# Three early expert rounds inside linear attention, resident weights and per-chunk gathers in a top-2 mixture-of-experts kernel

## The chip, the cores and the metric

The kernel runs on one core of one Trainium2 chip. The metric is device time in microseconds, lower is better. A median is given with the number of runs. A run is called slow when it is over 1.5% above the fastest of the same kernel; the ratios use the other runs, the fast ones.

## The reference, cut to what matters

```python
# attention: q, k, v of 8 batches x 8 heads x 576 x 64, phi(x) = elu(x) + 1
kv  = einsum('bhsd,bhse->bhde', phi(k), v);  z = sum(phi(k), axis=2)
x   = einsum('bhsd,bhde->bhse', phi(q), kv) / (einsum('bhsd,bhd->bhs', phi(q), z) + 1e-6)
x   = x.transpose(0, 2, 1, 3).reshape(4608, 512)
# noisy top-2 router over 8 experts, then the experts
noisy = x @ w_gate + log1p(exp(x @ w_noise)) * noise
top2, top2_w = the two best experts of each row and the softmax of their two values
for e in range(8):                                  # w1: 512 x 1024, w2: 1024 x 512
    out[rows of e] += weight * (relu(x[rows of e] @ w1[e]) @ w2[e])
```

Each of 4608 rows goes to two experts, so there are 9216 visits. The kernels give each expert ten tiles of 128 rows (1280 places), and a branch for overflow.

## The kernel before

It has two stages. The **attention stage** goes over four groups of two batches: cast loads of k, v, q on GpSimd, phi on ScalarE and VectorE, products and transposes on TensorE, routing (one step of it is the **ranking**, a few matmuls that give each row its place within its expert), and a **dispatch**: 18 scatters (indirect DMAs, issued by GpSimd) that write each row of x, with a few routing numbers, to the places of its two experts in the DRAM tensor `x_sorted`.

```python
# PhaseA.route, end: "dispatch"
for ci in range(NC):                 # 9 blocks of 128 rows
    for sl in range(2):              # first and second expert of a row
        r = nc.gpsimd.indirect_dma_start(out=self.x_sorted,
            out_offset=bass.IndirectOffsetOnAxis(ap=posi[:, ci, sl : sl + 1], axis=0),
            in_=xrow[:, ci, :].bitcast(INT32), in_offset=None)
```

The **expert stage** takes each expert's ten tiles in chunks of 4, 4 and 2. The two experts of a row both have to add into the same row of `out`. The second one to come therefore gathers what the first one wrote (called **L**), adds its own part while it empties the matmul bank, and scatters the sum. A gather may start only when all scatters of earlier experts have landed.

```python
# PhaseB.run; pools: 3 weight sets, 4 xt, 2 hT, 12 L, 6 y; PSUM 4 banks h, 3 banks y
for e in range(E):
    gate, si, gi = self.meta(...)                 # row data: where to gather and to scatter
    for n in (512, 512, 256):                     # a chunk: up to 4 tiles
        nc.sync.dma_start(out=xt[:, :, 0:n], in_=self.x_sorted[...], transpose=True)
        hT = self.mm1(w1, xt, n)                  # 32 matmuls, 8 ReLUs
        if prev is not None:
            flush(prev)                           # chunk before: 8 matmuls, y = ps*gate + L, scatter
        if t0 == 0:
            if e + 3 < E: self.load_w(e + 3)      # 4 loads of 512 KB, on GpSimd
            for t in range(T_CAP):
                L[t] = self.gather(gi[:, t : t + 1]) if e > 0 else None
        prev = {...}
```

## Time and profile before

| | before |
|---|---|
| time, median of 3 (range) | 583.14 us (580.96 to 592.49) |
| span of the first trace (a run of 597.23 us, 2.8% above the fastest of the three) | 595.4 us |
| attention stage, to the end of the last dispatch | 243.7 us |
| from there to the end | 351.7 us |
| TensorE busy, whole span | 373.5 us (63%) |

In the lines of the profile, L and a number is a source line, `a<-b` says what an instruction writes and reads, x and a number is a count. In a group the numbers after the bar are busy time in us and the mean of one instruction in ns; after the second bar stands how long the engine had idled just before these instructions, and what ended most of it. In a list of waits the three numbers are us in total, times, and the longest. In a timeline they are the start and the length in us, with the idle time before in brackets. In a table by stage, each engine's busy us and its instructions follow the stretch.

### The profile page before, as it was taken

Reading aid. Unit: us, or ns where it says so; the run is one execution under the profiler, and the core shown is the slowest. Engines: PE = TensorE matmul, PEld = TensorE weight load, DVE = VectorE, ACT = ScalarE, POOL = GpSimd, SP = SyncE. Lnnn points to the kernel's source line nnn. Section 1 sums busy time; section 2 is a strip of 40 time slices with the busy share of each in tenths; the row PEclk is TensorE's granted clock in tenths of the full one; section 3 lists DMA queues with packets and bytes.
Section 4 is the critical chain, followed back from the end, with each engine's and each line's share of the span. In section 5 each row is a group of like instructions: output and inputs, shape, how many; then the busy total and the mean of one; then the engine's idle time right before and its main releaser. Section 6 shows DMA issues by size and latency. Waiting matters only on the chain. (4 is left out here: it accounts for less than half of the span.)

```text
span 595.4 us, 5833 instructions
## 1 busy us (share of the span) xinstructions
PE 373.5 (63%) x1976; PEld 194.5 (33%) x1976; DVE 221.8 (37%) x638; ACT 170.2 (29%) x265; POOL 288.7 (48%) x315
## 2 busy tenths in 40 slices
PE   0173173137245300199989928969948968989984
PEld 0151142015124100045444404425424434444442
DVE  4359655375650560413233104314304304333122
ACT  0466444025021120062333401421511321423410
POOL 6445378427427117204346516725706726565364
PEclk9996555556555555589999978998987998998998
DMA  9999954995602002555864993993893995573153
GB/s 168 210 191 191 191 131 101 192 209 157 124 27 102 36 10 106 128 91 130 184 101 121 184 110 80 228 140 101 217 120 101 243 146 145 189 157 145 57 160 128
DMA packets 122985, 82.65 MB, mean 139 GB/s; under 512 B 74164, under 2 KB 108980, under 8 KB 122944
## 3 DMA queue, kind: packets, MB, share of 16 engines
q0 software_dynamic: 65888, 69.02, 56.8%
q1 hardware_dynamic: 54272, 12.98, 14.8%
q10 hardware_dynamic: 2784, 0.18, 0.4%
q8 instruction: 17, 0.28, 0.2%
q14 instruction: 24, 0.20, 0.1%
HBM read 80.72 MB, written 32.87 MB: 191 GB/s over the span
## 5 line engine op out<-in xcount | busy, mean ns | idle before, releaser
L474 PE MATMUL h_ps<-xt,w 128*128 128x512 bf16 (+1 forms) x768 | 150.5, 355 | 39.5 <-DMA xt<-x_sorted 32.3
L476 ACT ACTIVATE hT<-h_ps 128x512 bf16<-128x512 f32 (+1 forms) x192 | 99.4, 527 | 260.8 <-PE h_ps L474 209.2
L483 PE MATMUL y_ps<-w,hT 128*128 128x512 bf16 x640 | 149.8, 392 | 36.5 <-DVE y L489 36.5
L490 POOL DMA_INDIRECT out_dram<-y,si x80 | 79.4, 992 | 97.4 <-DVE y L487 39.9
L474 PEld LDWEIGHTS <-w 128*128 128x128 bf16 x768 | 77.8, 101 | 111.1 <-issue 46.9
L376 POOL DMA_INDIRECT x_sorted<-xrow,posi x72 | 73.6, 1022 | 78.9 <-DVE xrow L373 33.7
L461 POOL DMA_INDIRECT L<-out_dram,gi x70 | 70.6, 1009 | 82.1 <-DMA out_dram<-y,si 60.6
L483 PEld LDWEIGHTS <-hT 128*128 128x128 bf16 x640 | 64.1, 100 | 115.5 <-issue 45.3
L489 DVE SCALAR_TENSOR_TENSOR y<-y_ps,gate,L 128x512 f32<-128x512 f32 x70 | 51.1, 731 | 98.8 <-PE y_ps L483 60.6
L460 DVE MEMSET L<- 128x512 f32 x70 | 34.0, 485 | 34.4 <-DMA x_sorted<-xrow,posi 24.4
L270 PE MATMUL num_ps<-kvbd,pqt 128*128 128x162 bf16 x128 | 22.2, 324 | 38.6 <-DVE lwt L293 34.6
L203 PE MATMUL kv_ps<-v,phk 128*128 128x192 bf16 x128 | 26.0, 360 | 19.0 <-DVE phk L190 19.0
L335 PE MATMUL kv_ps<-A,ut 128*128 128x72 bf16 x4 | 0.9, 219 | 44.2 <-DVE A L331 44.2
L270 PEld LDWEIGHTS <-pqt 128*128 128x128 bf16 x128 | 13.2, 130 | 45.6 <-DVE lwt L293 41.3
L248 ACT COPY pqt<-t_ps 128x1024 bf16<-128x1024 bf16 x16 | 16.0, 1014 | 32.5 <-PE t_ps L244 10.6
L287 DVE TENSOR_TENSOR xrow<-num_ps,rden 128x512 bf16<-128x512 f32 x36 | 24.7, 687 | 0.5
L444 DVE SCALAR_TENSOR_TENSOR isf<-meta 128x10 f32<-128x10 f32 x8 | 1.4, 174 | 58.5 <-DMA meta<-x_sorted 58.5
L203 PEld LDWEIGHTS <-phk 128*128 128x128 bf16 x128 | 14.1, 131 | 23.6 <-DVE phk L190 19.0
L244 PE MATMUL t_ps<-ident,phq 128*128 128x128 bf16 x128 | 16.0, 306 | 8.0 <-ACT pqt L248 4.5
L185 ACT ACTIVATE e<-kt 128x2048 bf16<-128x2048 bf16 x8 | 15.2, 1912 | 10.7 <-DMA kt<-in_k_dram 7.9
L487 DVE TENSOR_SCALAR y<-y_ps,gate 128x512 f32<-128x512 f32 x10 | 7.5, 750 | 28.7 <-PE y_ps L483 28.7
L244 PEld LDWEIGHTS <-phq 128*128 128x128 bf16 x128 | 13.7, 144 | 9.2 <-issue 9.2
(116 smaller groups left out, 277.2 us busy)
## 6 DMA issues: line engine op xcount, KB each, us to landing
w<-in_moe_w_dram POOLq DMA_DIRECT2D x32, 512.0 KB
kt<-in_k_dram POOLq DMA_DIRECT2D x8, 512.0 KB
v<-in_v_dram POOLq DMA_DIRECT2D x8, 512.0 KB
qt<-in_q_dram POOLq DMA_DIRECT2D x8, 512.0 KB
x_sorted<-zrow SPq DMA_DIRECT2D x8, 264.0 KB, 6.6
out_dram<-y,si POOLq DMA_INDIRECT x80
x_sorted<-xrow,posi POOLq DMA_INDIRECT x72
L<-out_dram,gi POOLq DMA_INDIRECT x70
```

Source lines behind the costliest of these rows:

```text
L203: nc.tensor.matmul(out=ps[:, i, 0:192], lhsT=phk[:, hp, ci, :], rhs=vt[:, hp::4, 64 * ci : 64 * ci + 64], start=(i == 0 and ci == 0), stop ...
L244: nc.tensor.transpose(tp[:, i * 512 + ci * P : i * 512 + ci * P + P], phq[:, 2 * half + i, ci, :], c["ident"][:],)
L270: nc.tensor.matmul(out=ps[:, hp, 0:KVW], lhsT=pqs[j][:, hp, cc * P : cc * P + P], rhs=kvbds[j][:, hp, :], start=(hp % 2 == 0), stop=(hp % ...
L287: nc.vector.tensor_tensor(out=_ap(xrow[:, ci, 0:HD], [[64, 4], [256, 2], [1, 64]]), in0=_ap(ps, [[256, 4], [64, 2], [1, 64]]), in1=_ap(rd, ...
L376: r = nc.gpsimd.indirect_dma_start(out=self.x_sorted, out_offset=bass.IndirectOffsetOnAxis(ap=posi[:, ci, sl : sl + 1], axis=0), in_=xrow[ ...
L460: nc.vector.memset(L[:], 0.0)
L461: nc.gpsimd.indirect_dma_start(out=L[:].bitcast(INT32), out_offset=None, in_=self.out.bitcast(INT32), in_offset=bass.IndirectOffsetOnAxis( ...
L474: nc.tensor.matmul(out=ps[:, 0:n], lhsT=w1[:, dc, fc * P : fc * P + P], rhs=xt[:, dc, 0:n], start=(dc == 0), stop=(dc == 3))
L476: nc.scalar.activation(out=hT[:, fc, 0:n], in_=ps[:, 0:n], func=ACT.Relu)
L483: nc.tensor.matmul(out=ps[:], lhsT=hT[:, fc, t * P : t * P + P], rhs=w2[:, fc, :], start=(fc == 0), stop=(fc == 7))
L489: nc.vector.scalar_tensor_tensor(out=y[:], in0=ps[:], scalar=gate, in1=L[:], op0=ALU.mult, op1=ALU.add)
L490: r = nc.gpsimd.indirect_dma_start(out=self.out, out_offset=bass.IndirectOffsetOnAxis(ap=si, axis=0), in_=y[:], in_offset=None, bounds_che ...
```

## The change

The attention stage leaves TensorE mostly idle. The change wants to put expert work there: after three of six smaller routing units an **early round** does two tiles of each of experts 0 to 3, whose weights are loaded early and stay in SBUF. 24 of the 80 tiles move, and 56 are left for the **late stage**. To make room, the late stage also changes: L is gathered chunk by chunk into fewer buffers, there are two buffers for transposed rows (xt) and four for y, the second matmuls of a chunk are spread between the first matmuls of the next, and the weights of experts 4 to 6 are loaded when attention has ended. In attention the odd rows (512 to 575 of each head) are loaded on SP in fp32, and ScalarE's function table is loaded once.

```diff
+UNITS = [(0, 0, 4), (0, 4, 9), (1, 0, 9), (2, 0, 9), (3, 0, 4), (3, 4, 9)]
+ROUNDS = [(1, 256), (2, 512), (3, 768)]          # after unit 1, 2, 3; rows up to this bound
+    nc.scalar.preload_act_table_set(ACT_SET)
 ...  (PhaseB: pools)
-        self.wp = ctx.enter_context(tc.tile_pool(name="B_w", bufs=3))
-        self.xp = pool("B_x", 4)
-        self.lp = pool("B_l", 12)
-        self.yp = pool("B_y", 6)
+        self.wp = [pool("B_w", E1)]               # E1 = 4
+        self.xp = pool("B_x", 2)
+        self.lp = [pool("B_l", 3)]                # 3 more in the late stage
+        self.yp = [pool("B_y", 2)]                # 2 more in the late stage
 ...  (one chunk of an expert)
-                hT = self.mm1(w1, xt, n)
-                if prev is not None:
-                    flush(prev)
-                if t0 == 0:
-                    if e + 3 < E:
-                        self.load_w(e + 3)
-                    for t in range(T_CAP):
-                        L[t] = self.gather(gi[:, t : t + 1]) if e > 0 else None
+            self.mm1(w1, xt, hT, n, range(0, 2))
+            for i in range(1, 4):
+                want = -(-k * i // 4)
+                while done < want:
+                    self.tail(prev, done)         # second matmuls, y, scatter of the chunk before
+                    done += 1
+                self.mm1(w1, xt, hT, n, range(2 * i, 2 * i + 2))
+            while done < k: ...
+            L = {}
+            if not first:
+                for t in range(t0, t0 + n // P):
+                    L[t] = self.gather(gi[:, t : t + 1])
 ...  (main)
+        def early(i):
+            lo = ROUNDS[i - 1][1] if i else 0
+            for e in range(E1):
+                pb.expert(e, lo, (ROUNDS[i][1] - lo) // P, col(c["cnt"][i], e), i == 0 and e == 0, f"read{i}")
+            pb.flush()
+            if b < 2:
+                with tc.issue_after(pa.last_load):
+                    for e in ([0], [1, 2, 3])[b]:
+                        pb.load_w(e)
+            while unit < len(UNITS) and ...:
+                pa.route(unit)
+                for i, (after, _) in enumerate(ROUNDS):
+                    if after == unit:
+                        early(i)
+                unit += 1
+    for e in range(E1, 7):
+        pb.load_w(e, 1)
+    for e in range(E):
+        r0 = row0 if e < E1 else 0
+        pb.expert(e, r0, T_CAP - r0 // P, col(carry, e), False)
+        if e == 0:
+            pb.load_w(7)
```

## The prediction

> **What bounds the kernel now.** I read the engine table in 40 slices first, then busy time by stage (I cut the span at the four moments at which a group's ranking matmuls run and at the first expert matmul), then the groups, the waits, and the chain that ended last.
>
> ```profile
> PE   0173173137245300199989928969948968989984
> PEclk9996555556555555589999978998987998998998
> DMA  9999954995602002555864993993893995573153
> ```
>
> The attention half (slices 0 to 16) has TensorE mostly idle at half clock; the expert half has it nearly full. DMA is full only to about 75 us and again at 104 to 134 us, where the first three experts' weights load.
>
> ```profile
> core 0: us, PE busy (x) PEld busy (x) DVE busy (x) ACT busy (x) POOL busy (x), PEclk, DMA share, GB/s
> 0.00:72.40 72.40, 19.62 (x144) 13.24 (x145) 42.83 (x128) 32.23 (x29) 35.15 (x55) 0.84 1.45 190
> 72.40:128.00 55.60, 20.56 (x144) 13.43 (x143) 28.48 (x97) 17.19 (x18) 32.24 (x34) 0.50 0.89 154
> 128.00:171.90 43.90, 20.01 (x144) 12.84 (x143) 26.46 (x89) 12.53 (x14) 20.73 (x20) 0.54 0.56 123
> 171.90:218.90 47.00, 20.48 (x142) 13.16 (x140) 20.21 (x78) 8.82 (x12) 17.43 (x18) 0.50 0.14 52
> 218.90:251.10 32.20, 0.00 (x0) 0.01 (x1) 6.87 (x38) 0.00 (x0) 17.32 (x18) 0.50 0.35 99
> 251.10:595.40 344.30, 292.81 (x1408) 141.83 (x1408) 96.95 (x211) 99.41 (x192) 165.84 (x170) 0.92 0.68 143
> ```
>
> So: four attention groups of 72, 56, 44 and 47 us, no engine full, bound by chains from engine to engine (and by DMA in the first); 32 us in which only the last group's rows are scattered, TensorE at zero; then 344 us of experts, where TensorE is 293 us busy.
>
> ```profile
> L483 PE MATMUL y_ps<-w,hT 128*128 128x512 bf16 x640 | 149.8, 392 | 36.5 <-DVE y L489 36.5
> L490 POOL DMA_INDIRECT out_dram<-y,si x80 | 79.4, 992 | 97.4 <-DVE y L487 39.9
> L376 POOL DMA_INDIRECT x_sorted<-xrow,posi x72 | 73.6, 1022 | 78.9 <-DVE xrow L373 33.7
> L461 POOL DMA_INDIRECT L<-out_dram,gi x70 | 70.6, 1009 | 82.1 <-DMA out_dram<-y,si 60.6
> L489 DVE SCALAR_TENSOR_TENSOR y<-y_ps,gate,L 128x512 f32<-128x512 f32 x70 | 51.1, 731 | 98.8 <-PE y_ps L483 60.6
> PE y_ps L483 <- DVE y L489: 36.5, 6, 12.9
> POOL L L461 <- DMA out_dram<-y,si: 60.6, 6, 16.1
> ```
>
> An expert's partial results (L) may be gathered only when the scatters before have landed; 36.5 of TensorE's 51 idle us in the expert stage are that wait. In the chain that ended last, one of them is
>
> ```profile
> 473.96 8.41 DMA out_dram<-y,si
> ...
> 500.56 6.91 PE y_ps L483 x32
> ```
>
> The first line is a scatter issued just behind a weight load. Where no load is ahead, the timeline has a scatter landed 2.3 us after its issue ends, and a gather too. The second is the dense rate: 6.91/32 = 216 ns per 512-column matmul.
>
> **What the Trainium skill says.** "TensorE: Matmul & The Clock Gate", Part 1 and "Back-to-back issue gap": half rate by default and again after an idle window of about 3.4 us; N/2.4 + 2.5 ns warm. The trace agrees: 0.50 in attention, 216 ns when dense. "DMA: Bandwidth & Descriptors", "Issuing engines are not separate DMA queues": all queues use the same 16 engines, another issuer saves only issue time. No run here shows it yet. Same page, "Two DMAs through the same engine are not ordered": in one queue descriptors start in order; the 8.41 against 2.3 us fits a scatter queued behind a weight load. "ScalarE: Activation LUTs", "What ACT_TABLE_LOAD costs": about 1283 ns for the load itself; the trace has nine loads of 1283 ns.
>
> **The change, part by part.**
>
> *Expert work moved.* A tile of 128 rows costs 32 x 128 + 8 x 512 = 8192 columns, 16 x 216 ns = 3.45 us warm. There were and are 80 tiles. Three rounds x 4 experts x 2 tiles = 24 run early, 56 x 3.45 = 193 us remain. Removed from the late stage: 24 x 3.45 = 83 us.
>
> *Work added to the attention half.* POOL: 24 scatters and 22 gathers at 1.27 us (0.97 busy plus 0.3 between) = 58 us. DVE: 24 evictions x 0.75 = 18 us, 12 row-data blocks of nine instructions of about 0.17 = 18 us, two more routing units at some 9 us = 18 us; fewer, larger divisions give about 10 back. ACT: 96 ReLUs at 0.385 = 37 us and 22 zero copies at about 0.6 = 13 us, less eight table loads (10 us). Moving 24 odd-row loads from POOL to SP frees 24 x 0.7 = 17 us of POOL. DMA: 16 weight loads where 12 were; a 512 KB load at some 200 GB/s (209 in the slice at 119 us, nearly all weights) takes 2.6 us, so 42 us of queue, now in front of batches 3 and 4. No engine fills, but chains lengthen.
>
> *The new chain.* Two tiles per expert and round, one output bank, and L of expert e+1 gathered after the scatters of e: first eviction 0.75; second matmul block and eviction 2.7; scatter 0.8 + 1.0; landing 2.3; gather 1.0; landing 2.3: about 11 us per expert, 44 us per round, where its matmuls need 28 us warm (55 at half clock). In the instruction order of the changed kernel the ranking matmuls of units 2 and 3 stand in TensorE's queue behind most of a round: three experts' first matmuls and two experts' outputs. The queue is in order, so half a round, 22 to 28 us, is in the attention path, plus queueing of scatters between the next unit's 18 dispatches.
>
> *Timeline, in terms of a profiled run.* Round 0 needs unit 1 dispatched. In POOL's order 37 bulk loads and dispatches come before that dispatch: 27 or so bulk loads x 2.7 us, odd rows and zero fill about 25, 18 dispatches about 16, so it lands near 112, and rows are transposed 5 us later: 117 us. Unit 2 is ranked about 25 us on, at 142. The group after takes 44 (as before) + about 28 = 72: unit 3 at 214. Its 18 dispatches, with round 1's last scatters and gathers between them, take about 40, landing and transpose 7: round 2 starts at 261, takes 44, and unit 5 stands behind it: 305. Ten dispatches and some routing, 15: the last dispatch ends at 320, against 243.7 before. Subtracting a few us for overlap that I cannot see I use 317.
>
> *Late stage.* Landing and transpose 7 us (as before: 243.7 to 251.1). Matmuls 193. Twelve weight loads (experts 4 to 6) are issued just ahead of the first gathers: 12 x 2.6 = 31 us, while TensorE has 19 us of work before its three output banks are full: 10 us of wait, and about 7 more behind expert 7's load. After that gathers go per chunk, one round trip is about 9 us and TensorE has about 12 us of work: a few us of waits in all, 6. End: 7 us as now. Sum 7 + 193 + 23 + 7 = 230, against 351.7.
>
> Total 317 + 230 = 547 profiled, against 595.4. The timed median is 583.14/595.4 = 0.979 of the profiled span: 535 us, 8% faster. The late stage loses 122 us, the attention half gains 73.
>
> **The rivals.** (1) *Rounds hide well.* If TensorE goes warm in the rounds and scatters fill the gaps between dispatches, groups stay at 50 to 55 us and the last dispatch comes at 280: 500 us timed. For it: no engine is over half busy now. Against: one output bank and in-order queues. (2) *Rounds serialise.* If rounds do not overlap attention at all and TensorE stays at half clock (8 tiles x 6.9 = 55 us each), three rounds add 165 us, more than the late stage loses: 605 us or so. For it: the present groups wait on engine after engine. Against: the order interleaves the ends of each round with the next batch. (3) *DMA becomes the bound*: weights and zero fill delay batches 3 to 5, rounds start at 130 to 140: 550 to 560. For it: DMA was already full to 75 us. Against: it has long holes after 150 us. (4) *Late stage as patchy as now* (51 of 344 us idle): 56 tiles with 15% idle give 228 us instead of 216, so 12 us more: 547.
>
> **Range and chances.** The late stage is the safer half: 220 to 245. The last dispatch is the uncertain number: 280 to 345. Both ends rarely meet, so 500 to 575 timed. Slower than 571 needs attention to grow by over 110 us, near rival 2: 12% in all, a third of it beyond +2%. Faster by over 2%: 0.88; same 0.08; slower 0.04.
>
> **What would show the steps right or wrong.** The last dispatch near 317 us; from it to the end about 230. TensorE idle in the late stage about 25 us, mostly one wait on the first gathers behind weights. In each round, gathers that wait for scatters 2 to 4 us at a time, experts about 11 us apart. POOL at 55 to 60% of the span, clock in the attention half between 0.5 and 0.8. The ranking waits for expert matmuls rather than for DVE alone. Wrong if rounds take over 60 us, if batches 3 to 5 wait for k, v or q data long after 120 us, or if the late stage waits for L in every chunk.

## The result, and the profile after

The changed kernel is slower: 659.78 us (median of 4 runs, 657.85 to 663.67) against 586.54 us (median of 4) for the kernel before. The ratio is 1.134, 95% interval 1.125 to 1.144. A ratio here is the mean time of one kernel's fast runs over that of the other's fast runs in the same rounds, so not quite the ratio of the medians quoted.

The page of the changed kernel, in 40 slices of its 656.0 us (16.4 us each):

```profile
PE   0323370377841686438830046669987979979850
PEclk9999996578965799659955588789997998989895
DMA  9999999992446622344212999644434255354341
```

TensorE is now busy in parts of slices 7 to 20. But the last dispatch ends only at 360.2 us, at the end of slice 21 (counted from 0). TensorE is nearly idle in slices 21 and 22, and DMA is full in slices 22 to 24. Steady expert work starts only near slice 27.

Groups and waits of the changed kernel, the ones that answer to those shown of before:

```profile
L535 PE MATMUL y_ps<-w,hT 128*128 128x512 bf16 x611 | 164.3, 408 | 62.5 <-DVE y L541 59.8
L542 POOL DMA_INDIRECT out_dram<-y,si x80 | 80.7, 1009 | 124.7 <-DVE y L541 46.5
L515 POOL DMA_INDIRECT L<-out_dram,gi x78 | 79.8, 1023 | 108.1 <-DMA out_dram<-y,si 45.0
L541 DVE SCALAR_TENSOR_TENSOR y<-y_ps,gate,L 128x512 f32<-128x512 f32 x78 | 57.7, 742 | 190.3 <-DMA L<-out_dram,gi 119.2
...
PE h_ps L527 <- DMA xt<-x_sorted: 79.9, 5, 30.0
PE y_ps L535 <- DVE y L541: 59.8, 20, 8.6
```

The work per instruction is as before. The waits grew: TensorE waits 59.8 us for y in 20 places, where it was 36.5 us in 6, and 79.9 us for transposed rows, where the kernel before has one such wait of 32.3 us. VectorE waits 119.2 us for L.

The stages, from the changed kernel's table of stretches (cut at ranking matmuls and at the last dispatch):

```profile
83.95:163.31 79.36, 43.70 (x311) 29.36 (x314) 32.85 (x116) 25.33 (x47) 25.67 (x28) 0.74 0.97 160
163.31:248.26 84.95, 50.97 (x401) 32.88 (x406) 35.97 (x124) 34.27 (x69) 40.90 (x40) 0.80 0.49 106
248.26:276.32 28.06, 13.49 (x111) 7.83 (x111) 17.30 (x60) 7.00 (x15) 19.50 (x20) 0.76 0.30 104
276.32:345.66 69.34, 41.46 (x288) 25.82 (x293) 21.95 (x85) 19.14 (x47) 29.79 (x30) 0.77 0.31 86
...
360.20:656.00 295.80, 209.39 (x941) 97.16 (x959) 73.16 (x169) 69.59 (x128) 124.71 (x128) 0.87 0.54 125
```

The late stage takes 295.8 us for 56 tiles, of which TensorE is busy 209. In the timeline, the late stage starts like this on TensorE:

```profile
375.98 8.43 PE L527 MATMUL h_ps<-xt,w 128*128 128x512 bf16 x32 [30.00 <-DMA xt<-x_sorted]
396.00 2.29 PE L527 MATMUL h_ps<-xt,w 128*128 128x512 bf16 x5 [11.60 <-DMA xt<-x_sorted]
...
415.37 3.57 PE L535 MATMUL y_ps<-w,hT 128*128 128x512 bf16 x8 [8.56 <-DVE y L541]
```

The first late scatter is issued at 415.6 us, 55 us after the last dispatch. Later, GpSimd goes through a four-tile chunk like this:

```profile
479.30 1.04 POOL L515 DMA_INDIRECT L<-out_dram,gi  x1 [3.56 <-DMA out_dram<-y,si]
...
483.28 1.00 POOL L515 DMA_INDIRECT L<-out_dram,gi  x1 [0.30 <-issue]
487.19 1.02 POOL L542 DMA_INDIRECT out_dram<-y,si  x1 [2.91 <-DVE L L512]
...
491.09 0.97 POOL L542 DMA_INDIRECT out_dram<-y,si  x1 [0.30 <-issue]
495.13 1.04 POOL L515 DMA_INDIRECT L<-out_dram,gi  x1 [3.07 <-DMA out_dram<-y,si]
```

Four gathers, a wait for them and for what follows, four scatters, a wait for their landing, and then the next four gathers: 495.13 - 479.30 = 15.8 us for four tiles, where TensorE needs 4 x 3.45 = 13.8.

### The profile page after: what moved, and what is told of

Read it like the earlier page. It is cut to its first block, busy times and chain, and to the rows that moved or that the text cites. A ratio compares the mean times of both kernels' runs of the same rounds, so it can differ in the third digit from the quotient of the medians.

```text
span 656.0 us, 6607 instructions
## 1 busy us (share of the span) xinstructions
PE 380.6 (58%) x2231; PEld 207.4 (32%) x2266; DVE 222.6 (34%) x694; ACT 184.1 (28%) x341; POOL 282.6 (43%) x307
## 5 line engine op out<-in xcount | busy, mean ns | idle before, releaser
L527 PE MATMUL h_ps<-xt,w 128*128 128x256 bf16 (+1 forms) x890 | 168.5, 335 | 82.3 <-DMA xt<-x_sorted 79.9
L535 PE MATMUL y_ps<-w,hT 128*128 128x512 bf16 x611 | 164.3, 408 | 62.5 <-DVE y L541 59.8
L529 ACT ACTIVATE hT<-h_ps 128x256 bf16<-128x256 f32 (+1 forms) x224 | 105.4, 475 | 271.2 <-PE h_ps L527 261.7
L527 PEld LDWEIGHTS <-w 128*128 128x128 bf16 x896 | 92.3, 103 | 153.9 <-issue 95.8
L541 DVE SCALAR_TENSOR_TENSOR y<-y_ps,gate,L 128x512 f32<-128x512 f32 x78 | 57.7, 742 | 190.3 <-DMA L<-out_dram,gi 119.2
L425 POOL DMA_INDIRECT x_sorted<-xr,posi x72 | 71.8, 997 | 56.0 <-DMA w<-in_moe_w_dram 21.2
L201 ACT ACTIVATE e<-kq 128x2048 bf16<-128x2048 bf16 x16 | 30.4, 1909 | 59.4 <-DMA kq<-in_k_dram 36.9
L239 PE MATMUL misc<-v,ph 128*128 128x192 bf16 x128 | 23.0, 317 | 18.7 <-DVE tm L215 18.7
L321 DVE TENSOR_TENSOR xr<-num,rden 128x512 bf16<-128x512 f32 x36 | 23.5, 685 | 3.6 <-PE num L295 1.7
L205 DVE TENSOR_TENSOR ph<-e,kq 128x1024 bf16<-128x1024 bf16 x32 | 21.2, 683 | 4.7 <-PE misc L275 3.3
L239 PEld LDWEIGHTS <-ph 128*128 128x128 bf16 x128 | 12.3, 118 | 22.4 <-DVE tm L215 18.6
L291 PE MATMUL num<-kvbd,pqt 128*128 128x128 bf16 x128 | 16.2, 271 | 3.1 <-DVE xr L321 3.1
## 6 DMA issues: line engine op xcount, KB each, us to landing
kq<-in_k_dram POOLq DMA_DIRECT2D x8, 512.0 KB, 17.1
```

The lines of the kernel that those rows point to most:

```text
L201: nc.scalar.activation(out=e[:], in_=flat, func=ACT.Exp)
L239: nc.tensor.matmul(out=ps[:, i, 0:192], lhsT=phk[:, hp, ci, :], rhs=vt[:, hp::4, 64 * ci : 64 * ci + 64], start=(i == 0 and ci == 0), stop ...
L291: nc.tensor.matmul(out=out, lhsT=pqt[:, hp, ci * P : ci * P + P], rhs=kvbds[-1][:, hp, cols], start=start, stop=stop, skip_group_check=True)
L321: nc.vector.tensor_tensor(out=_ap(xr[:, ci, 0:HD], [[64, 4], [256, 2], [1, 64]]), in0=_ap(ps, [[128, 4], [64, 2], [1, 64]]), in1=_ap(rden[ ...
L425: r = nc.gpsimd.indirect_dma_start(out=self.x_sorted, out_offset=bass.IndirectOffsetOnAxis(ap=posi[:, ci - c0, sl : sl + 1], axis=0), in_= ...
L527: nc.tensor.matmul(out=ps[:, 0:n], lhsT=w1[:, dc, fc * P : fc * P + P], rhs=xt[:, dc, 0:n], start=(dc == 0), stop=(dc == 3))
```

## The experiments

The theory at this point had three parts: the early rounds gain nothing because attention grows by as much; the late stage starts late because twelve weight loads stand in front; per-chunk gathers slow its pace. 18 kernels ran. Runs 5 and 7 give a wrong result. The kernel before was timed again on the same chip, and chips differ (its median was 582.6 to 600.1 us), so ratios are used. How far to trust them: the kernel before against itself, run 13, came out at 0.994 (0.983 to 1.004). Here "last dispatch" and "first scatter" (the first scatter of the stage after it) are times in the run's own trace.

| run | last dispatch ends | first scatter | span of trace | median | ratio to before |
|---|---|---|---|---|---|
| before, first trace | 243.7 | 271 | 595.4 | 583.14 | 1 |
| changed kernel | 360.2 | 415.6 | 656.0 | 659.78 | 1.134 |
| e1 whole-expert gathers | 358 | 414 | 641.2 | 642.79 | 1.091 |
| e2 weights later | 360 | 416 | 663.0 | 667.14 | 1.133 |
| e3 both | 359 | 406 | 639.2 | 643.63 | 1.092 |
| e4 no rounds | 242 | 289 | 650.1 | 650.32 | 1.099 |
| e5 no late weights | 364 | 385 | 621.0 | 619.13 | 1.066 |
| e6 = e1 + weights ordered | 359 | 379 | 623.5 | 626.55 | 1.080 |
| e7 no gathers | 336 | | 584.4 | 586.21 (one run) | |
| e8 = e6 without rounds | 242 | 262 | 595.7 | 605.59 | 1.046 |
| e9 = e6, rounds behind ranking | 360 | 382 | 635.4 (slow) | 625.37 | 1.053 |
| e10 before, weights moved | 250 | 277 | 581.9 | 580.57 | 0.980 |
| e11 before, table preloaded | 242 | 268 | 591.2 | 597.77 | 1.006 |
| e12 = e10 + e11 | 243 | 269 | 576.9 | 576.83 | 0.971 |
| e13 before again | 229.0 | 255 | 578.3 | 579.74 | 0.994 |
| e14 = e8, weights behind gathers | 243 | 263 | 592.4 | 595.00 | 1.019 |
| e15 = e8, buffers as before | 242 | 263 | 579.8 | 579.78 | 0.993 |
| e16 = e8, not spread | 243 | 269 | 598.7 | 597.14 | 1.021 |
| e17 = e15 with rounds | 362 | 385 | 619.0 | 623.43 | 1.043 |
| e18 = e15 + e14 + e16 | 263 | 289 | 627.9 | 626.83 | 1.044 |

**Run 1, whole-expert gathers.**

```diff
-            L = {}
-            if not first:
-                for t in range(t0, t0 + n // P):
-                    L[t] = self.gather(gi[:, t : t + 1])
+            if t0 == 0 or not self.late:
+                L = {}
+                if not first:
+                    for t in range(t0, nt if self.late else t0 + n // P):
+                        L[t] = self.gather(gi[:, t : t + 1])
-    pb.lp.append(right("B_l2", 3))
+    pb.lp = [right("B_l2", 12)]
```

> One edit to the changed kernel: in the late stage all of an expert's partial results are gathered at once after its first chunk (12 buffers), as in the kernel before; the early rounds are untouched. Theory (per-chunk gathers make GpSimd alternate gathers and scatters, each waiting for the other's landing): the 10-tile experts, 41 to 42 us each now, come down to about 38 (34.5 dense plus the 4.6 us that the kernel before lost per expert), the 4-tile experts stay, since for them a chunk is the whole expert: 4 x 3.5 = 14 us less, about 646 us. Rival (the gathers are hidden anyway and the pace is set by scatter landing): within 5 us of 660.

642.79 us, 17 us less (15 us by the spans of the traces, 1.134 to 1.091 by the ratios), with the start unchanged: first scatter 56 us after the last dispatch. The theory holds: per-chunk gathers cost 15 to 17 us by these times; the ratios would make it about 25.

**Runs 2 and 3, weights later in the program.** Run 3 is run 1 with this edit.

```diff
-    for e in range(E1, 7):
-        pb.load_w(e, 1)
...
-        if e == 0:
-            pb.load_w(7)
+        if e < 4:
+            pb.load_w(4 + e, 1 if e < 3 else 0)
```

> One edit to the changed kernel: the weights of experts 4, 5, 6 are loaded one expert at a time after experts 0, 1, 2 instead of all twelve loads just before the first late gathers. Theory (the twelve loads delay the first transposes, row data and gathers): the first late matmul comes 7 to 9 us after the last dispatch instead of 15.8, the 30.0 and 11.6 us waits for xt shrink to under 10, the start-up loss of about 50 us falls to about 20, and the time to about 630. Rival (the start-up is the latency of row data, gather and scatter itself, or the loads only move to a later place in the same queue and delay scatters there): 650 to 660.

> The edits of the two runs before together. Theory: the gains add, 14 + 30 = 44 us, about 616 us, still slower than the kernel before (587), because the attention half stays at 360 us. Rival: weights spread over experts 0 to 3 meet the gathers, and the sum is under 25 us: 635 or more.

667.14 and 643.63 us: no gain over the changed kernel and over run 1. By the text of the two expectations the rival wins (667.14 lies even above its range). But the traces show that the edits did not do what they were made for: the scheduler issued ten of the sixteen loads ahead of the first late scatter all the same (14 in the changed kernel; the "eight" in the expectation of run 5 is a miscount), and the first scatters came at 416 and 406 us. So they do not tell whether the loads make the start; run 5 was made for that. They do show one thing: in run 2 only two loads stood in front of the first four gathers and eight right behind them, and still the first two transposes took 17.8 and 27.8 us to land. Moving loads behind the gathers was not enough here.

**Run 4, no early rounds.**

```diff
-ROUNDS = [(1, 256), (2, 512), (3, 768)]
+ROUNDS = []
```

> The changed kernel with no early round at all; everything else (six units, rows of the odd part on SP in fp32, resident weights, late stage with per-chunk gathers) is kept. Theory (the three rounds lengthen attention by about as much as they save later): last dispatch at about 255 instead of 360, late stage 80 tiles at 4.15 us plus 64 of start and end, about 395: total about 650, within 15 us of the changed kernel. Rival A (the rounds are what costs the 13%): 600 or less. Rival B (the rounds do pay, as I predicted, and the loss is all in the late stage): 690 or more.

650.32 us, as the theory had it in total; its two parts missed by 13 us each in opposite directions (last dispatch at 242 instead of 255, late stage 408 instead of 395). Its stages are:

```profile
83.89:140.89 57.00, 18.17 (x179) 13.03 (x179) 26.45 (x74) 15.98 (x21) 18.02 (x20) 0.64 1.14 188
140.89:187.33 46.44, 17.00 (x182) 11.85 (x182) 26.04 (x75) 15.46 (x20) 21.91 (x22) 0.61 0.53 109
187.33:207.03 19.70, 10.11 (x86) 6.69 (x86) 13.69 (x50) 4.27 (x10) 13.23 (x14) 0.50 0.27 96
207.03:227.44 20.41, 10.38 (x101) 7.18 (x101) 11.55 (x44) 4.36 (x10) 11.98 (x13) 0.58 0.27 96
...
242.00:650.00 408.00, 306.56 (x1408) 144.05 (x1407) 103.02 (x219) 100.89 (x192) 173.09 (x177) 0.87 0.51 118
```

The stretches of attention that took 79.36, 84.95 and 69.34 us with rounds take 57.00, 46.44 and 20.41 us without. In all the three rounds move the last dispatch from 242.0 to 360.2 us, 118.2 us, and shorten the late stage from 408.0 to 295.8 us, 112.2 us. The rounds are worth nothing here; by the ratios, which take the chips into account, the kernel is even 3% better off without them. Between the second ranking and the last one, TensorE was busy 18.17 + 17.00 + 10.11 + 10.38 = 55.7 of 143.6 us without rounds, so idle for 87.9; with them it was busy 43.70 + 50.97 + 13.49 + 41.46 = 149.6 of 261.7 us, so idle for 112.1. The rounds filled none of the idle time that they were meant to fill.

**Run 5, no late weight loads.**

```diff
-    pb.wp.append(right("B_w2", 3))
-    for e in range(E1, 7):
-        pb.load_w(e, 1)
+    for e in range(E1, E):
+        pb.w[e] = pb.w[e - E1]
-        if e == 0:
-            pb.load_w(7)
```

> Wrong result on purpose: the changed kernel with the sixteen late weight loads taken out; experts 4 to 7 use the weights of experts 0 to 3 that are in SBUF already. Nothing else changes. Run 2 moved the loads in the program, but the scheduler still issued eight of them ahead of the first late scatter, so it did not test the start. Theory (the twelve loads in front of transposes and row data make the start): first late matmul 7 to 9 us after the last dispatch (15.8 in the changed kernel), first late scatter 25 us after it instead of 55, and with no later loads about 620 us in all. Rival (row data, transposes and the first gathers are slow by themselves): first scatter still 45 us or more after the last dispatch, 645 or more.

619.13 us, first scatter 21 us after the last dispatch instead of 55. The theory holds. The list of DMA issues in the first 60 us of the late stage shows why; the last number is the median from issue to landing. First the changed kernel, then run 5:

```profile
w<-in_moe_w_dram POOLq DMA_DIRECT2D x14, 512.0 KB, 18.0
...
L<-out_dram,gi POOLq DMA_INDIRECT x4, 18.4
xt<-x_sorted SPq DMA_TRANSPOSE x3, 13.6
```

```profile
L<-out_dram,gi POOLq DMA_INDIRECT x12, 2.7
...
xt<-x_sorted SPq DMA_TRANSPOSE x6, 4.5
```

In the median a gather behind the loads took 18.4 us and one without loads 2.7. The transposes, which another engine issues, took 13.6 instead of 4.5.

**Run 6, gathers and weights both repaired.** Run 1, with the loads forced behind scatters:

```diff
-    for e in range(E1, 7):
-        pb.load_w(e, 1)
...
+        if 1 <= e <= 4:
+            with tc.issue_after(pb.last_sc):      # last scatter of expert e - 1
+                pb.load_w(3 + e, 1 if e < 4 else 0)
```

> Whole-expert gathers as in run 1, and the loads of experts 4, 5, 6, 7 forced in GpSimd's queue behind the last late scatter of experts 0, 1, 2, 3. Correct. Theory (start made by the loads): first late scatter about 25 us after the last dispatch, 25 to 30 us less than run 1: about 615 us. Rival (the loads cost the same wherever they stand, because each gather then waits behind them): 635 or more.

626.55 us, between the two expectations. The first scatter comes 20 us after the last dispatch, so the start is repaired by 36 us against run 1; but only 18 us of it are left in the span (641.2 to 623.5), and 1% in the ratio (the chips differ). The rest is lost further on: in this run the loads stand among the gathers and scatters of experts 0 to 4.

**Run 7, no gathers.**

```diff
-            if not first:
+            if False:
...
-            out=self.out, out_offset=...
+            out=dst, out_offset=...               # a scratch tensor for each expert
...
+    with tc.issue_after(pb.last_x):
+        for i in range(N_TOK // P):
+            nc.sync.dma_start(out=out[i * P : i * P + P, :], in_=c["zero"][:])
```

> Wrong result on purpose: no expert gathers anything, each expert scatters to a scratch tensor of its own, and the output is filled with zeros near the end. Only the last dispatch and the pace between are to be read, not the total. Theory (the chain scatter, landing, gather, landing inside each round is what lengthens attention by 118 us against run 4): last dispatch at 300 us or earlier. Rival (the rounds' matmuls, ReLUs and evictions stand in the in-order queues of TensorE, ScalarE and VectorE in front of the next unit's work, gathers or not): 335 or later. In the late stage, once started, both expect the dense pace of 34.5 to 36 us per ten tiles.

The last dispatch ends at 336 us (a single run, so its state is unknown). The rival wins: of the 118 us that three rounds cost, the chains of scatter, landing, gather and landing account for 24 at most. A variant that leaves out only the early gathers could not be run, because two experts' writes to one row would race; that is why all gathers went, and why the experts write to tensors of their own.

**Run 8, no rounds, late stage repaired.** Run 6 with `ROUNDS = []` and no gathers for the first expert.

> No early rounds, whole-expert gathers, none for the first expert, and weight loads of experts 4 to 7 forced behind the scatters of experts 0 to 3. Correct. Theory (the late stage of the change lost to per-chunk gathers and to loads in front of the start, the rounds gained nothing): last dispatch at 242, then a late stage like the 352 us of the kernel before: 585 to 600 us, within 2% of the kernel before. Rival (other parts of the change cost too: two xt buffers, four y buffers, tails spread between first matmuls): 615 or more.

The trace looks like the kernel before (242 and 353.7 us against 243.7 and 351.7), but its time was the fastest of four. The ratio is 1.046 (1.034 to 1.057; two of the four runs were slow), between the two expectations. So there was a rest, and the four runs 13 to 16 look for it.

**Run 9, rounds behind the ranking.** In the changed kernel TensorE stands at the head of each round and waits, with attention work behind it in its queue. The timeline shows the first matmul of each round:

```profile
128.55 1.86 PE L527 MATMUL h_ps<-xt,w 128*128 128x256 bf16 x8 [9.67 <-DMA xt<-x_sorted]
...
217.96 2.29 PE L527 MATMUL h_ps<-xt,w 128*128 128x256 bf16 x10 [18.51 <-DMA xt<-x_sorted]
...
289.70 6.78 PE L527 MATMUL h_ps<-xt,w 128*128 128x256 bf16 x40 [10.12 <-DMA xt<-x_sorted]
```

```diff
-                    if after == unit:
-                        early(i)
+                    if after + 1 == unit:
+                        with tc.issue_after(pa.last_rank):   # ranking matmul of the next unit
+                            early(i)
```

> Run 6 with one edit: each early round is queued on TensorE behind the ranking matmuls of the next unit, instead of standing in its in-order queue while its rows are still being scattered and transposed (9.7, 18.5 and 10.1 us of waits for xt at the heads of the three rounds in the changed kernel). Correct. Theory (what the rounds cost beyond their matmuls is TensorE standing at the head of a round with attention work queued behind it): last dispatch at 325 us or earlier instead of 359, total about 595. Rival (the rounds' own TensorE work, about 94 us by the busy times of runs 4 and the changed kernel, is simply in series with attention wherever it stands): last dispatch 345 or later, 610 or more.

The waits at the heads of the first two rounds fell to 2.9 and 4.8 us and the fourth unit (unit 3) was ranked 27 us earlier, at 221 us. But then the other two rounds ran one after the other from 257 us on, the last unit was ranked only at 338 us, and the last dispatch ended at 360 us again. The rival wins: the 35 us that the theory needed did not come, and the rounds stand in series with attention in this place too. That the new place gains nothing is not shown. The profiled run was a slow one (637.65 us; the fast ones took 622.73 to 625.37), and its trace has 24 us of VectorE waits before the last dispatch whose releaser is not in the core's records (see run 13). By the fast runs the ratio is 1.053 (1.039 to 1.068) where run 6 has 1.080 (1.069 to 1.092) on another chip, so some 15 us may have been won.

**Runs 10, 11 and 12, the kernel before with the lessons.** Run 10 moves the weight loads:

```diff
+        self.wp2 = pool("B_w2", 3)                # in the expert stage
+        wp = self.wp2 if 3 <= e <= 5 else self.wp
...
-                    if e + 3 < E:
-                        self.load_w(e + 3)
                     for t in range(T_CAP):
                         L[t] = self.gather(gi[:, t : t + 1]) if e > 0 else None
+                    if 1 <= e <= 5:
+                        with self.tc.issue_after(self.last_g):   # behind the tenth gather
+                            self.load_w(e + 2)
```

Run 11 only adds `nc.scalar.preload_act_table_set("natural_log_exp_and_others")`, and run 12 does both.

> The kernel before, with the weight loads moved from among an expert's scatters to right behind its ten gathers, into three more weight buffers opened in the expert stage. Correct. Theory (a scatter that lands late because it was issued behind a weight load holds up the next expert's gathers; 8.41 us in the chain of the kernel before against 2.3 us without a load ahead): TensorE's 36 us of waits at the expert boundaries fall to about 20, the time by 10 to 20 us, to 568 to 576. Rival (the loads then delay the gathers' landings and the first scatters by as much): within 5 us of the kernel before.

> The kernel before with one part of the change alone: the ScalarE function table is preloaded once with a set that holds exponential and logarithm. Correct. The kernel before has nine table loads of 1283 ns; most stand in the routing chains. Theory: each routing chain loses one to two loads, 1.3 to 3 us, four groups: 5 to 10 us faster, about 577 us. Rival (the loads lie in ScalarE's idle time): within 3 us.

> The edits of the two runs before together: the version that should beat both kernels. Theory: the gains add, 15 + 7 = 22 us: about 562 us, 3 to 4% faster than the kernel before. Rival (either edit hidden): 570 or more.

Run 10: ratio 0.980 (0.972 to 0.988), some 12 us and so within the 10 to 20 expected; the waits of TensorE for y, 36.5 us in the kernel before, are 3.3 us in its trace. It moved the loads and added weight buffers at once; which of the two did it was not separated. Run 11: 1.006 (0.994 to 1.018), so the rival holds: no gain from the table shows. Run 12: 0.971 (0.962 to 0.981; 3 to 4% faster was expected), faster than both kernels. Its expert stage:

```profile
242.50:576.90 334.40, 291.19 (x1384) 142.72 (x1408) 96.60 (x223) 98.26 (x192) 164.32 (x171) 0.95 0.64 150
```

334.4 us, where the first trace of the kernel before has 351.7. Whether the preload adds anything to run 10's gain is within the intervals of the two.

**Run 13, the kernel before again**, unchanged.

> The kernel before, unchanged, for a second trace. If run 8 and the kernel before differ in the late stage, this trace shows the expert stage shorter than the 351.7 us of the first trace, by about 10 us; if they differ in attention, the last dispatch comes before 243.7 us. If it only repeats the first trace, the rest of run 8 stays open.

The attention stage ends at 229.0 us, not 243.7; the expert stage is 349.3 us. Most of the difference of the two traces, 13.3 of 17.1 us, lies in the fourth group, where the first trace has a stop that this one lacks:

```profile
199.49 1.93 ACT L248 COPY pqt<-t_ps 128x1024 bf16<-128x1024 bf16 x2 [10.19 <-remote]
```

ScalarE idled 10.19 us, and what released it is not in the core's records (the profile calls this "remote"). Sums of such waits, as used below, are not lost time: they add several engines, so that one stop can count twice (VectorE's 7.6 us at 199.65 us are this same stop), and they include idle time that the engine would have had anyway. Some may be no stops at all: the eight traces without such waits have a matmul record for every weight load, and all traces with such waits, apart from this first one, lack 24 to 35 matmul records, so the releaser may be one of those.

**Runs 14, 15 and 16, the rest of run 8**, one edit each:

```diff
 e14
-            with tc.issue_after(pb.last_sc):
+            with tc.issue_after(pb.last_g):
 e15
-    pb.wp.append(right("B_w2", 3))
+    pb.wp.append(right("B_w2", 2))                # one weight set less, for room
-    pb.yp.append(right("B_y2", 2))
+    pb.yp = [right("B_y2", 6)]
+    pb.xp = right("B_x2", 4)
 e16
-            self.mm1(w1, xt, hT, n, range(0, 2))
-            for i in range(1, 4): ...             # second matmuls spread between first ones
+            self.mm1(w1, xt, hT, n, range(8))
```

> Run 8 with one edit: the weight loads stand behind the ten gathers of experts 1 to 4 instead of among their last scatters, as in run 10. Theory (scatters landing late behind loads hold up the next gathers): 10 to 18 us less than run 8, ratio to the kernel before about 1.02. Rival: within 4 us of run 8.

> Run 8 with one edit: in the late stage four buffers for transposed rows and six for y, as in the kernel before (the change has two and four). Theory (fewer buffers cost the rest): 10 us or more below run 8. Rival (buffers are not the limit, TensorE had 1 us waits for xt at most in run 8's late stage): within 4 us of run 8.

> Run 8 with one edit: the second matmuls of the chunk before are done after all first matmuls of a chunk, as in the kernel before, instead of between them. Theory (spread second matmuls need L earlier and stop the first matmuls when it is late): 8 us or more below run 8. Rival: within 4 us of run 8, or slower since spreading was meant to give scatters time.

The ratios are 1.019, 0.993 and 1.021 where run 8 had 1.046. The buffers are the largest part, and with them the kernel is level with the one before (0.985 to 1.001); which of the two, xt or y, was not tested. Waits of TensorE in run 8, then in run 15:

```profile
PE y_ps L535 <- DVE y L541: 40.1, 11, 4.6
```

```profile
PE y_ps L535 <- DVE y L541: 27.8, 8, 7.2
```

The late stage shrinks from 353.7 to 337.8 us. The other two edits gained about 2.5% each by their ratios, but their spans (592.4 and 598.7 us) are within 3.3 us of run 8's profiled run, which was its fastest, so their gain is less sure.

**Runs 17 and 18.** Run 17 is run 6 with the buffers of run 15, so it is run 15 with the three rounds (and a gather for the first expert). Run 18 is run 15 with the edits of runs 14 and 16.

> The changed kernel with its three rounds and all late repairs: whole-expert gathers, weight loads in order behind the scatters of experts 0 to 3, four xt and six y buffers. It differs from run 15 in the rounds alone. Theory (24 early tiles lengthen attention by 118 us and save about 24 x 4.0 = 96 us): last dispatch at 359, late stage about 245, total 600 to 608, 20 to 28 us slower than run 15. Rival (the rounds pay when the late stage is sound): 580 or less.

> Run 15 with the edits of runs 14 and 16 as well: no rounds, whole-expert gathers, weight loads behind the gathers, four xt and six y buffers, second matmuls not spread. Theory: late stage like run 12's 334 us, last dispatch at 242: about 575 us, 1 to 2% faster than the kernel before. Rival (the edits overlap: each removes the same waits as the buffers do): within 4 us of run 15.

Run 17: 1.043 (1.033 to 1.052) against run 15's 0.993 on another chip, and the last dispatch at 362 us against 242. As the theory had it, the rounds lose also with a sound late stage, 5% here: they lengthen attention by 120 us and shorten the late stage from 337.8 to 257.0 us, by 81. Run 18 at 1.044 contradicts both of its expectations. Its trace has 17 waits, 79.6 us in all, whose releaser is not in the core's records, like the one shown in run 13, and its attention stage ends at 263 us where run 15's ends at 242; run 15's trace has no such wait. Run 18 ran on another chip, with run 17, and says nothing sure about its edits.

## Why the prediction was wrong

The prediction was 535 us with a chance of 0.88 for faster; it came 13% slower. In the terms of the profiled sum, 547 became 656.0, 109 us more: 43 in the attention half (last dispatch at 360.2 instead of 317) and 66 in the late stage (295.8 instead of 230).

- **The step that failed most is "half a round, 22 to 28 us, is in the attention path".** Against run 4, the ranking of unit 2 came 22.4 us later (163.31 against 140.89), that of unit 3 another 38.5, that of unit 5 another 57.3: 118.2 in all, where the sum had allowed 73 between the kernel before and the changed one. Only the first of the three lies within the 22 to 28. In the prediction's own timeline the largest miss is the first: unit 2 was put at 142 us, "about 25 us on" from a round 0 that starts at 117; it came at 163.31, because round 0 began at 128.55 and 34.8 us passed from there (142 us is about what run 4 has with no round at all). The group after took 84.95 us where 72 were allowed, and from the start of round 2 to the last ranking passed 56.0 us where 44 were allowed.
- **A round was longer than "44 us per round" as well.** From its first matmul to the end of its last scatter the three took 72, 60 and 52 us, the first of them past the prediction's own sign of failure, "over 60 us".
- **The rival "rounds serialise"** was right about the mechanism. The size that I gave it (165 us, all at half clock) was too large: with the rounds TensorE was busy for 94 us more, near the 83 us of 24 tiles at full rate. Its "605 us" is also a wrong sum: 595.4 + 165 - 122 is 638 profiled, about 625 by the same factor.
- **Why they serialise** is shown only in part. Gathers give 24 us of the 118 (run 7). Waiting at the head of a round is not the main part: with most of these waits removed, the last dispatch came no earlier in the trace of run 9, though its fast runs leave room for some 15 us. TensorE's 94 us (149.6 - 55.7) are most of the 118. That the rest of each batch waits behind a round's matmuls, ReLUs and evictions in three in-order queues fits, but it is not shown: no run separates the three.
- **"10 us of wait and about 7 more" for the start of the late stage.** The mechanism was in the prediction, the twelve loads in front of the first gathers, but only their effect on L was counted. The transposed rows and row data waited as well, though SP issues them: first matmul 15.8 us after the last dispatch instead of 7, first scatter 55 us after it. Without loads it is 21 us (run 5), so the term was 34 us. This is what the Trainium skill says ("DMA: Bandwidth & Descriptors", "Issuing engines are not separate DMA queues"), which I quoted and did not apply; the trace agrees with 13.6 against 4.5 us for a transpose.
- **"One round trip is about 9 us and TensorE has about 12 us of work: a few us of waits, 6".** The pieces were right, but GpSimd issues four gathers and four scatters in one queue, 9.9 us, and two waits of 2.9 and 3.1 us come on top in series: 15.8 us for a four-tile chunk. Whole-expert gathers take back 17 us (run 1), four xt and six y buffers another 16 (353.7 to 337.8 us, runs 8 and 15). The prediction had noted neither pool. Its sign of failure, "if the late stage waits for L in every chunk", is what happened. With all these repairs the late stage is 257.0 us (run 17), still 27 above the predicted 230; what the rest is stays open.
- **The factor 0.979** from profiled to timed was wrong too. It came from one profiled run that was 2% slow, and run 13 shows the kernel before at 578.3 us. Timed is span plus 1.9 us. That alone moves 535 to 549.
- **What held:** 3.45 us per tile (run 7's late stage has ten tiles in 34.6 us), the experts of a round about 11 us apart (10 to 14 us in round 2), and GpSimd's 1.3 us per indirect DMA. One reading was uneven: 8.41 us for a landing behind a load counts from the start of the issue, 2.3 us from its end; counted alike it is 8.41 against 3.3.

The 77.7 us between two undisturbed traces (656.0 and 578.3) are thus: 13.0 for attention without rounds (242.0 against 229.0), 118.2 for the rounds, 58.7 for a slower late stage at the same 80 tiles (408.0 against 349.3), less 112.2 for the tiles moved. The 13.0 were not tested alone; expert weights loaded from 30 us on, among the batch data, are one candidate.

## What to carry to other kernels

An engine's idle time need not be room for other work: here the work moved into it left TensorE idle for longer than without it (112.1 us for 87.9), probably because it goes through the same in-order queues as the chain that leaves the engine idle. So first run the kernel with the extra work taken out and compare how much idle time really went. Keep bulk loads away from the front of latency-bound transfers and from the last scatters that the next gathers wait for: with an expert's four loads right behind its ten gathers, and three weight sets more, the kernel before was 2% faster (run 10). Being behind the gathers is not enough where row data and transposes still have to land (run 2). When buffers are cut to make room for a new overlap, time the kernel with the smaller buffers and without the overlap.

## What the Trainium skill lacked or had wrong

- "DMA: Bandwidth & Descriptors": the section on issuing engines says that all queues share the engines, but gives no size for what a small transfer loses beside bulk loads. Here, with 14 loads of 512 KB in the first 60 us, a gather took 18.4 us instead of 2.7 in the median and a transpose from another queue 13.6 instead of 4.5.
- "TensorE: Matmul & The Clock Gate": Part 1 has half rate after an idle window of about 3.4 us. Run 12 seems to contradict it and does not, so nothing is wrong with the page here: run 12's profile gives a granted clock of 1.00 through an attention stage with idle stretches up to 16 us, where that of the kernel before gives 0.50. But eight 128-column transposes took 1.01 us in both, against 0.61 us in run 13 at 182.6 us, with a granted clock of 1.00; and run 12's trace holds no clock record at all before 254 us. Its 1.00 is a gap in the record and not a speed. (The page warns that such records can be unreliable.)
- No page has it: waits of up to some 15 us whose releaser is not in the core's records, 26.6 us in all in the first trace of the kernel before, 33 to 80 us in the traces of runs 9 to 12, 17 and 18, and 0 to 5.4 us in all others. Apart from the first trace they came with two chips, where the kernel before was slower too (median 597.6 and 600.1 us against 582.6 to 591.0). What they are is open, and how much of these sums is real lost time too (see run 13).
